# Two one-bank PSUM tiles for the products in place of the halves of one two-bank tile, and a new order of the first products

## The chip, the core and the metric

The kernel runs on one core of a Trainium2 chip. Its engines are TensorE (PE; its weight loads are shown apart as PEld), VectorE (DVE), ScalarE (ACT), GpSimd (POOL) and SyncE (SP, which here issues DMAs). The metric is the device time of one execution in microseconds (us). The measurement of this kernel repeats to about 0.2%.

## The reference

One call computes three things in fp32: attention in which a query sees only the keys of its hash bucket (2 batches, 8 heads, 768 positions, 64 wide), and two feed-forward blocks over 1536 tokens of width 512.

```
# attention: scores where the 6-bit buckets of q and k agree, else -1e9; softmax; times v
# first block (d_ff 1024)
a = x @ w1;  b = x @ w2
h = a * b @ w3
out_1 = h @ w_out
# second block (d_ff 1536)
g = x @ w_gate
silu = g * (1.0 / (1.0 + exp(-g)))
val = x @ w_val
out_2 = silu * val @ w_out
```

## The kernel before, in words

**Order of the work.** The kernel is written as small operations, each with candidate engines, an estimated cost, a priority and resources that it takes and gives back (slots of SBUF, PSUM tiles, temporaries). A planner (`Plan`) walks a model of time when the program is built, chooses an engine for each operation and fixes the order of each engine's queue. Semaphores are then put in by tile: an instruction that writes a tile waits for earlier readers of that tile and the like. Engines work their queues in order, so an instruction that waits holds back all behind it on its engine. TensorE's operations are chained in the order in which the code names them (`fill_op`), so the planner does not reorder products.

**Stages.** The attention fills the span to about 317 us, mixed with first pieces of the two blocks; until about 463 us the first third of the tokens goes through both blocks, and weights prepared there are kept in DRAM. Then `pair` handles the other two thirds together: `pair(1, ...)` the first block (about 463 to 598 us) and `pair(2, ...)` the second (598 to 797 us). The change works in these two calls.

**Exact products from fast ones.** An fp32 product is made of three fast matmuls on high and low parts (`split_mm`, L248 to L251). A *group* is such a triple: 128 weights columns, 512 columns moved. A low part is written by DVE or POOL at L262, a high part by ACT at L255.

**Sets.** In `pair` the tokens and weights are combined in the manner of Strassen: for each pair of column blocks `jp` and each `z` of 0 and 1 there is a *set* of seven products p1 to p7, of two groups each (q = 0 and 1), in place of eight. The first call has four `jp` (8 sets), the second six (12 sets). `wset` fetches two weight blocks (wA, wB) from DRAM and forms two sums of them (wP, wQ): two full adds (L1156), four quarter adds (L1167) on DVE or POOL, then high and low parts. `xset` does the like for the tokens (X1.., X2..; T1 to T4 are sums).

**Banks of the products.** Products accumulate in PSUM: p1 and p2 in tile `a`, p6 in `b` (one bank each, from two tiles tagged "one"). `cd` is one tile of 128x1024, two banks, one of three tagged "two"; p5 and p3 use its first half ("bank c"), p7 and p4 its second ("bank d"). After each product `after` has an eviction of 128x512 put out: ACT copies `a` to `u` (L1349); DVE adds `b` to `u`, then c to `u` gives `v` (p5), d to `v` gives part of G (p7), c to `u` (p3) and d to `u` (p4), all at L1321. Accumulation goes on: p3 adds to what p5 left in c, p4 to what p7 left in d, so p3 must wait for the eviction of p5, p4 for that of p7, and the next set's p5 and p7 for the evictions of p3 and p4. Products of G (L1334) and their splits (C) feed the second stage: *units* of one group on tiles `pacc`, of which `some` puts one behind p6, p2, p7 and p3 each, so that a regular set is p1 p6 unit p5 p2 unit p7 unit p3 unit p4, 54 matmuls. In the first set of a call there are no units yet, except that the first call begins with four units of the work before it (`lead`, tile `acc`; copies `ot` at L1083 take them out and a DMA stores each).

The order of the first two sets of a call is written out by hand in `pair`; before it is, as z then p: 01 11 02 12 05 07 06 16 03 04 15 17 13 14.

Of the kernel before, what the change touches and what calls it, by code (L numbers as in the profile page):

```python
# [28 lines left out]
NSLOT_MOE = 14  # L29
# [3 lines left out]
N_ST = 7  # L33
# [138 lines left out]
def moe_after_bucket_attention(ctx: ExitStack, tc: tile.TileContext, qk, vv, pp, cst, w12, w3t, w_out, wgv, wo2, out):  # L172
# [4 lines left out]
    psum = ctx.enter_context(tc.tile_pool(name="psum", bufs=1, space=bass.MemoryType.PSUM))  # L177
    ctx.enter_context(tc.manual_schedule())
    pools = {}
# [28 lines left out]
    env = {}  # L208
    uid = [0]

    def two(key):
        env[key] = psum.tile([128, 1024], F32, tag="two", name=key, bufs=3)
        return env[key]
# [225 lines left out]
    def head(hh):  # L439
# [74 lines left out]
        def bits():  # L514
            r = slice(QB0, KB0 + NM)
            DVE.tensor_scalar(  # L516
                out=q[r], in0=env.pop(f"proj{hh}")[r, 0:S], scalar1=thr[r], scalar2=val[r], op0=ALU.is_gt, op1=ALU.mult
            )
# [7 lines left out]
        def bits_k():  # L526
            r = slice(QB0, QB0 + NM)
            DVE.tensor_scalar(
                out=k[r], in0=env.pop("projk")[r, 0:S], scalar1=pr[r, 14:15], scalar2=pr[r, 15:16],
# [52 lines left out]
    def tile_ops(s):  # L582
# [11 lines left out]
        def clip():  # L594
            env[f"ms{s}"] = ap.tile([128, S], F32, tag="ms", name=f"ms{s}", bufs=N_MS)
            env[f"mx{s}"] = ap.tile([128, 2], F32, tag="mx", name=f"mx{s}", bufs=6)
            ps = env.pop(f"S{s}")
# [28 lines left out]
        def pe_second():  # L626
            v = env.pop(f"T{s}")[:, 0:S].rearrange("p (c q) -> p c q", c=6)
# [392 lines left out]
    def stage2(n, cdep):  # L1020
# [11 lines left out]
        for o_ in range(4):  # L1032

            def go(o_=o_):
                if first and at[o_][1] == 0:
                    two(ak + str(at[o_][0]))
# [25 lines left out]
            if kind == 1:  # L1062
# [13 lines left out]
            else:  # L1076

                def e1(eng, o_=o_):
                    def go():
# [155 lines left out]
    def pair(kind, nj, xdep, lead, gate, prio):  # L1235
# [8 lines left out]
        for jp in range(njp):  # L1244
            for z in range(2):
                w_of[jp, z] = wset(f"{kind}_{jp}_{z}", f"{kind}_{2 * jp}_{z}", f"{kind}_{2 * jp + 1}_{z}")
            if kind == 2:
                for j in (2 * jp, 2 * jp + 1):
                    wo_of[j] = fetch(f"wo2p_{j}", f"2_{j}_2", 1)
        if kind == 2:  # L1250
            for j in range(nj):
                wo_of[j, 2] = fetch(f"wo2q_{j}", f"2_{j}_2", 1)

        def prod(jp, z, p):
            key = f"{kind}_{jp}_{z}"
            wn, c0, xn = PROD[p]
            bank = {1: "a", 2: "a", 6: "b", 5: "c", 3: "c", 7: "d", 4: "d"}[p]
            begins = p in (1, 6, 5, 7)
            o = None
            for q in range(2):  # L1260

                def go(q=q):
                    if bank in "ab":
                        if begins and q == 0:
                            one(bank + key)
                        ps = env[bank + key]
# [14 lines left out]
                if begins and q == 0:  # L1281
                    if bank in "ab":
                        acq = [("F", 1)]
                    elif bank == "c":
                        deps.append(cd[0])
                        if cd[2] != kind:
# [19 lines left out]
        def after(jp, z, p, o):  # L1306
# [10 lines left out]
            def cdb(h):  # L1317
                return env["cd"][:, HALF[h]]
# [69 lines left out]
            elif p == 4:  # L1388
                rel = []
                if jp == njp - 1:  # L1390
                    rel = [("two", 1)]

                def go():
# [224 lines left out]
```

## Time and profile before

| | |
|---|---|
| median of 3 runs | 804.15 us (803.67 to 805.5) |
| profiled execution | 803.58 us, of which the span from first to last instruction is 801.8 us |
| mean granted TensorE clock | 0.997 |
| busy: PE, PEld, DVE, ACT, POOL | 761.0, 624.9, 539.3, 486.3, 332.9 us |
| matmul instructions | 3888 |

Read it as follows. Busy shares are means over stages of different limits; a busy TensorE counts overlapped durations, so the count of matmuls in a stretch tells more than the busy time. In the timeline a bracket behind a row gives the idle time before it on that engine and what ended it. Rows of 128x512 matmuls overlap: their starts stand closer together than they are long.

### The profile page before, as it was taken

The page shows a single profiled execution, that of the slowest core. Times are in us where ns is not written, and L with a number is a line of the kernel's source. Part 1 is how long each engine was busy: PE and PEld are TensorE (multiplying, and loading weights), DVE is VectorE, ACT ScalarE, POOL GpSimd, SP SyncE. Part 2 cuts the span into 40 slices and gives each one's busy share as a digit, 9 for nine tenths or more (in the row PEclk, how much of TensorE's full clock was granted, in tenths as well). Part 3 has the DMA queues.
Part 4 walks back from the last instruction along what each step waited for, and adds up shares of the span by engine and source line. Part 5 has one row for each costly group of instructions (what it writes and reads, how often), then busy time and mean ns, then how long its engine had stood idle before and what let it go on. Part 6 is the DMA issues. An engine that isn't in the chain of part 4 may idle for free.

```text
span 801.8 us, 11300 instructions
## 1 busy us (share of the span) xinstructions
PE 761.0 (95%) x3888; PEld 624.9 (78%) x3888; DVE 539.3 (67%) x929; ACT 486.3 (61%) x880; POOL 332.9 (42%) x321
## 2 busy tenths in 40 slices
PE   7998999999999899999999998999997899999997
PEld 5786888888888789787888875777785677777786
DVE  7888878878778987274378665566646675565450
ACT  7988989998789899698898832122332322322210
POOL 3676578575547553245421434232206123252000
PEclk9999999999999999999999999999999999999999
DMA  7794955774696862798888862212242333354211
GB/s 216 171 229 119 221 162 142 152 186 117 175 230 193 237 202 71 272 324 302 310 312 313 292 226 89 82 58 81 99 131 80 105 105 102 109 163 151 105 52 54
DMA packets 43329, 135.11 MB, mean 169 GB/s; under 512 B 7892, under 2 KB 10068, under 8 KB 43272
## 3 DMA queue, kind: packets, MB, share of 16 engines
q1 hardware_dynamic: 41032, 123.38, 48.3%
q0 software_dynamic: 2240, 11.01, 6.6%
q8 instruction: 31, 0.51, 0.3%
q14 instruction: 26, 0.21, 0.1%
HBM read 97.85 MB, written 30.46 MB: 160 GB/s over the span
## 4 chain that ended last, share of the span: by engine, by line
PE 67%; DVE 13%; ACT 8%; issue 5%; DMA 4%; POOL 2%; SPq 0%; POOLq 0%; ACTq 0%; DVEq 0%
PE cd L249 6%; PE T L620 5%; PE cd L251 4%; PE cd L250 4%; PE av L689 3%; PE av L690 3%; DVE sl_G L1321 3%; PE pacc_two L249 2%; PE pacc_two L251 2%; PE pacc_two L250 2%; PE S L591 2%; PE S L592 2%; PE a L249 2%; PE a L251 2%; PE a L250 2%
## 5 line engine op out<-in xcount | busy, mean ns | idle before, releaser
L598 DVE TENSOR_SCALAR_CACHE_REDUCE ms<-S 128x768 f32<-128x768 f32 x96 | 91.3, 951 | 20.5 <-PE S L592 13.8
L262 DVE TENSOR_TENSOR P<-T,P 128x768 fp32r<-128x768 f32 x96 | 91.0, 953 | 18.9 <-ACT P L624 18.1
L611 ACT ACTIVATE ms<-ms,mx 128x768 f32<-128x768 f32 x96 | 89.8, 936 | 6.2 <-DVE mx L605 5.7
L620 PE MATMUL T<-cs,ms 128*128 128x128 f32 x576 | 79.3, 274 | 3.3 <-ACT ms L611 1.0
L624 ACT CAST P<-T 128x768 fp32r<-128x768 f32 x96 | 76.1, 796 | 7.0 <-PE T L620 5.4
L689 PE MATMUL av<-P,VP 128*128 128x256 f32 x288 | 75.8, 297 | 0.6 <-ACT tt L700 0.3
L620 PEld LDWEIGHTS T<-cs,ms 128*128 128x128 f32 x576 | 65.3, 141 | 11.6 <-ACT ms L611 3.5
L690 PE MATMUL av<-P,VP 128*128 128x256 f32 x288 | 72.6, 286 | 0.8 <-DVE P L262 0.8
L591 PE MATMUL S<-KQ 128*128 128x512 f32 x192 | 67.8, 357 | 3.0 <-DVE ms L598 0.9
L592 PE MATMUL S<-KH,QL 128*128 128x512 f32 x192 | 60.5, 338 | 0.7 <-DVE QL L516 0.7
L689 PEld LDWEIGHTS av<-P,VP 128*128 128x128 f32 x288 | 55.4, 192 | 2.7 <-ACT tt L700 1.8
L690 PEld LDWEIGHTS av<-P,VP 128*128 128x128 f32 x288 | 55.6, 193 | 1.6 <-DVE P L262 1.2
L1349 ACT COPY u<-a 128x512 f32<-128x512 f32 x20 | 11.7, 586 | 72.0 <-PE a L251 71.9
L1167 POOL TENSOR_TENSOR sl_F<-sl_F 128x256 f32<-128x256 f32 x17 | 12.8, 756 | 84.8 <-DVE sl_F L1167 84.4
L262 POOL TENSOR_TENSOR sl_w2x<-sl_raww2x,sl_w2x 128x512 fp32r<-128x512 f32 x20 | 27.1, 1360 | 50.1 <-ACT sl_w2x L255 47.1
L255 ACT ACTIVATE dec_w2x<-sl_raww2x 128x512 f32<-128x512 f32 (+1 forms) x64 | 45.0, 728 | 3.9 <-DVE sl_raww2x L360 3.4
L591 PEld LDWEIGHTS S<-KQ 128*128 128x128 f32 x192 | 36.1, 188 | 12.1 <-DVE ms L598 3.2
L592 PEld LDWEIGHTS S<-KH,QL 128*128 128x128 f32 x192 | 36.2, 189 | 6.2 <-DVE QL L516 1.1
L360 DVE SCALAR_TENSOR_TENSOR sl_raww2x<-dec_w2x,dec_w2x 128x512 uint32<-128x512 uint32 x36 | 27.5, 764 | 16.9 <-ACT dec_w2x L255 16.2
L249 PE MATMUL m<-sl_X,sl_w2x 128*128 128x512 f32 x96 | 37.5, 390 | 1.4 <-ACT sa_m L902 1.4
L251 PE MATMUL m<-sl_X,sl_w2x 128*128 128x512 f32 x96 | 37.4, 389 | 0.0
L250 PE MATMUL m<-sl_X,sl_w2x 128*128 128x512 f32 x96 | 37.3, 389 | 0.0
(277 smaller groups left out, 2234.0 us busy)
## 6 DMA issues: line engine op xcount, KB each, us to landing
dram<-sl_w2x SPq DMA_DIRECT2D x36, 512.0 KB, 3.7
sl_raww2x<-in_wgv_dram SPq DMA_DIRECT2D x24, 512.0 KB, 6.2
KQ<-in_qk_dram POOLq DMA_DIRECT2D x28, 384.0 KB, 6.3
sl_wA<-dram SPq DMA_DIRECT2D x20, 512.0 KB, 4.2
sl_wB<-dram SPq DMA_DIRECT2D x20, 512.0 KB, 3.4
sl_raww<-in_w3t_dram SPq DMA_DIRECT2D x16, 512.0 KB, 4.8
sl_raww12f<-in_w_dram SPq DMA_DIRECT2D x16, 512.0 KB, 4.3
dram<-sl_w12f SPq DMA_DIRECT2D x16, 512.0 KB, 5.8
```

What stands on the lines that cost most here:

```text
L249: PE.matmul(ps, a_hi, b_hi, start=first, stop=False, skip_group_check=more)
L250: PE.matmul(ps, a_hi, b_lo, start=False, stop=False, skip_group_check=more)
L251: PE.matmul(ps, a_lo, b_hi, start=False, stop=last, skip_group_check=more)
L262: eng.tensor_tensor(out=out_, in0=a, in1=b, op=ALU.subtract)
L591: PE.matmul(ps[:, c0:c1], a[:, 0, qs], a[:, 1, c0:c1], start=True, stop=False)
L592: PE.matmul(ps[:, c0:c1], q[:, qs], k[:, c0:c1], start=False, stop=True)
L598: DVE.tensor_scalar(out=env[f"ms{s}"], in0=ps[:, 0:S], scalar1=-BIG, scalar2=None, op0=ALU.max, op1=ALU.max, accum_out=env[f"mx{s}"][:, 0:1],)
L611: ACT.activation(p, p, AF.Exp, bias=m[:, 1:2], scale=0.125, accum_out=env[f"sums{hh}"][:, qt : qt + 1])
L620: PE.transpose(ps[:, c * 128 : c * 128 + 128], p[:, c * 128 : c * 128 + 128], ident)
L624: ACT.copy(env[f"P{n}"][:, kk, 0:6], env[f"T{s}"][:, 0:S].rearrange("p (c q) -> p c q", c=6))
L689: PE.matmul(ps[:, 0:256], vab, p[:, :, c], start=c == 0, stop=False)
L690: PE.matmul(ps[:, 0:256], vab, p[:, :, 6 + c], start=False, stop=c == 5)
```

## The change

- `cd` is no longer one tile of two banks. The third of the "two" tiles lies in a pool of its own; when the first product on bank c comes, that pool is closed and a new one is opened in its place with two tiles of one bank, `c` and `d` (`bank_pair`, `bank`). They stay to the end of the second call.
- The "two" tiles are given out from an explicit list; accumulators that last never get the third.
- In the second call the units of the last pass use `c` and `d` in place of a "two" (`at1`).
- The products of the first two sets (first call) or the first four (second call, where two `jp` are interwoven) stand in a new order. The lead units of the first call follow the first product; before, they followed the third.
- Fetches of the second block's output weights are named behind the next `jp`'s weights; there are 15 slots for 14, and 5 temporaries for 7 (`N_ST`).

```diff
-NSLOT_MOE = 14
+NSLOT_MOE = 15
-N_ST = 7
+N_ST = 5
...
+    psum_c = tc.tile_pool(name="psum_c", bufs=1, space=bass.MemoryType.PSUM)
+    pools = {"two0": psum, "two1": psum, "two2": psum_c.__enter__()}
...
+    def bank_pair():
+        free_twos.remove("two2")
+        psum_c.__exit__(None, None, None)
+        pools["cd"] = ctx.enter_context(tc.tile_pool(name="psum_cd", bufs=1, space=bass.MemoryType.PSUM))
+
+    def bank(which, key):
+        env[key] = pools["cd"].tile([128, 512], F32, tag=which, name=key, bufs=1)
         return env[key]
...
-                        if "cd" not in env:
-                            two("cd")
-                        ps = env["cd"][:, HALF[bank == "d"]]
+                        if "cd" not in pools:
+                            bank_pair()
+                        if at not in env:
+                            bank(at, at)
+                        ps = env[at]
...
             def cdb(h):
-                return env["cd"][:, HALF[h]]
+                return env["cd"[h]]
...
-        at1 = [("one", 0, 0), ("one", 1, 0), ("two", 0, 0), ("two", 0, 1)]
+        at1 = [("one", 0, 0), ("one", 1, 0), *([("two", 0, 0), ("two", 0, 1)] if kind == 1 else [("c", 0, 0), ("d", 0, 0)])]
...
-                order = [(0, 1), (1, 1), (0, 2), (1, 2), (0, 5), (0, 7), (0, 6), (1, 6), (0, 3), (0, 4), (1, 5), (1, 7), (1, 3), (1, 4)]
+        if kind == 1:
+            seq = steps(0, "01 06 05 07 02 11 03 16 04 15 12 17 13 14 01' 06' 02' 05' 07' 03' 04' 11' 16' 15' 12' 17' 13' 14'")
+        else:
+            seq = steps(0, "01 11 02 12 01' 11' 02' 05 07 06 12' 16 03 04 15 17 06' 13 14 05' 07' 03' 04' 16' 15' 17' 13' 14'")
```

(A stroke marks the second `jp`.) What the change moves, in the order of three places; of each group only the first matmul stands, and "waits" names the engine whose semaphore is waited for.

TensorE in the first two sets of the first call, before: from the p3 of the first set on. `X1..` are parts of the tokens, `w..` of the weights.

```order
L249 MATMUL cd<-sl_X1B_166_4887,sl_wP_0_0_214_5412 128x512 [waits DVE_49]
...
L249 MATMUL cd<-sl_X1B_168_4897,sl_wP_0_0_214_5412 128x512 [waits DVE_49]
...
L249 MATMUL cd<-sl_X1T_197_5218,sl_wB_0_0_206_5324 128x512 [waits DMAHW7_49]
...
L249 MATMUL cd<-sl_X1T_198_5224,sl_wB_0_0_206_5324 128x512 [waits DVE_49]
...
L249 MATMUL cd<-sl_X1T_175_4985,sl_wQ_0_1_222_5494 128x512 [waits Activation_49]
...
L249 MATMUL cd<-sl_X1T_180_5032,sl_wQ_0_1_222_5494 128x512 [waits DVE_49]
...
L249 MATMUL cd<-sl_X1T_181_5034,sl_wQ_0_1_222_5494 128x512
...
L249 MATMUL cd<-sl_X1T_186_5097,sl_wQ_0_1_222_5494 128x512 [waits DVE_49]
```

Now, from the same p3 on:

```order
L268 MATMUL c<-sl_X1B_166_4890,sl_wP_0_0_215_5417 128x512 [waits DVE_49]
...
L268 MATMUL c<-sl_X1B_168_4900,sl_wP_0_0_215_5417 128x512
...
L268 MATMUL b_0_1_5519<-sl_X1T_190_5144,sl_wP_0_1_220_5491 128x512 [waits Activation_49]
...
L268 MATMUL b_0_1_5519<-sl_X1T_191_5154,sl_wP_0_1_220_5491 128x512
...
L268 MATMUL d<-sl_X1T_195_5191,sl_wB_0_0_206_5319 128x512 [waits DMAHW7_49]
...
L268 MATMUL d<-sl_X1T_199_5233,sl_wB_0_0_206_5319 128x512
...
L268 MATMUL c<-sl_X1T_175_4988,sl_wQ_0_1_223_5511 128x512 [waits DVE_49,Activation_49]
...
L268 MATMUL c<-sl_X1T_181_5037,sl_wQ_0_1_223_5511 128x512
...
L268 MATMUL a_0_1_5498<-sl_X1B_162_4844,sl_wA_0_1_209_5356 128x512 [waits Activation_49]
...
L268 MATMUL a_0_1_5498<-sl_X1B_163_4864,sl_wA_0_1_209_5356 128x512
...
L268 MATMUL d<-sl_X1T_182_5052,sl_wQ_0_1_223_5511 128x512 [waits DVE_49]
...
L268 MATMUL d<-sl_X1T_186_5102,sl_wQ_0_1_223_5511 128x512
```

The products of c and d stood next to each other, with a wait ahead of a second group, too (the sl_wP, wB and wQ rows with a wait in the middle of a product); now products on `a`, `b`, `c` and `d` take turns, and a wait stands only ahead of a product's first group.

VectorE in the same sets, before: from the low part of the first wP on.

```order
L262 TENSOR_TENSOR sl_wP_0_0_214_5412<-sl_F_0_0_209_5355,sl_wP_0_0_214_5412 128x512 [waits Activation_49]
L262 TENSOR_TENSOR sl_wQ_0_0_216_5434<-sl_F_0_0_209_5355,sl_wQ_0_0_216_5434 128x512 [waits Activation_49]
L1167 TENSOR_TENSOR sl_F_0_1_215_5414<-sl_F_0_1_215_5414 128x256 [waits DMAHW4_49,Pool_49]
L1167 TENSOR_TENSOR sl_F_0_1_215_5414<-sl_F_0_1_215_5414 128x256 [waits DVE_49] x3
L1321 TENSOR_TENSOR sl_G_1_0_217_5440<-a_0_1_5416,sl_G_1_0_217_5440 128x512 [waits PE_49,Activation_49]
L262 TENSOR_TENSOR sl_wP_0_1_220_5477<-sl_F_0_1_215_5414,sl_wP_0_1_220_5477 128x512 [waits DMAHW0_49,Activation_49]
L262 TENSOR_TENSOR sl_C1p_0_221_5488<-sl_G_1_0_217_5440,sl_C1p_0_221_5488 128x512 [waits Activation_49]
L262 TENSOR_TENSOR sl_wQ_0_1_222_5494<-sl_F_0_1_215_5414,sl_wQ_0_1_222_5494 128x512 [waits Activation_49]
```

Now, from the same low part on:

```order
L281 TENSOR_TENSOR sl_wP_0_0_215_5417<-sl_F_0_0_210_5363,sl_wP_0_0_215_5417 128x512 [waits Activation_49]
L1106 COPY ot_1_5434<-acc_0_0_4581 128x512 [waits Activation_49]
L281 TENSOR_TENSOR sl_wQ_0_0_216_5436<-sl_F_0_0_210_5363,sl_wQ_0_0_216_5436 128x512 [waits DMAHW4_49,DMAHW0_49,Activation_49]
L1190 TENSOR_TENSOR sl_F_0_1_214_5411<-sl_F_0_1_214_5411 128x256 [waits Pool_49]
L1190 TENSOR_TENSOR sl_F_0_1_214_5411<-sl_F_0_1_214_5411 128x256 [waits DVE_49]
L1348 TENSOR_TENSOR u_0_0_5422<-b_0_0_5443,u_0_0_5422 128x512 [waits PE_49]
L1106 COPY ot_3_5475<-acc_0_1_4594 128x512 [waits DMAHW6_49,Activation_49]
L1348 TENSOR_TENSOR v_0_0_5477<-c,u_0_0_5422 128x512 [waits DVE_49,PE_49]
L1348 TENSOR_TENSOR sl_G_1_0_219_5489<-d,v_0_0_5477 128x512 [waits DMAHW0_49,DVE_49,PE_49]
```

Two of the four copies `ot` of the lead units, which ACT made before, stand on VectorE now, the second with a wait for a DMA; behind it stand the evictions of p5 (`v`) and p7. The eviction of p6 (`u`) has moved up ahead of the next set's splits.

TensorE at the head of the second call, before (of each product the first matmul):

```order
L249 MATMUL a_0_0_6315<-sl_X2B_288_6214,sl_wA_0_0_258_5944 128x512 [waits DMAHW5_49,Activation_49]
...
L249 MATMUL a_0_1_6327<-sl_X2B_288_6214,sl_wA_0_1_267_6035 128x512 [waits DMAHW7_49,Activation_49]
...
L249 MATMUL a_0_0_6315<-sl_X2B_291_6231,sl_wA_0_0_258_5944 128x512 [waits Activation_49]
...
L249 MATMUL a_0_1_6327<-sl_X2B_291_6231,sl_wA_0_1_267_6035 128x512 [waits Activation_49]
...
L249 MATMUL cd<-sl_X2T_293_6270,sl_wQ_0_0_275_6104 128x512 [waits DVE_49]
...
L249 MATMUL cd<-sl_X2T_298_6339,sl_wQ_0_0_275_6104 128x512 [waits DVE_49]
...
L249 MATMUL b_0_0_6388<-sl_X2T_302_6371,sl_wP_0_0_272_6082 128x512 [waits Activation_49]
...
L249 MATMUL b_0_1_6404<-sl_X2T_302_6371,sl_wP_0_1_281_6181 128x512
...
L249 MATMUL cd<-sl_X2B_296_6324,sl_wP_0_0_272_6082 128x512 [waits DVE_49]
...
L249 MATMUL cd<-sl_X2T_306_6395,sl_wB_0_0_264_6006 128x512 [waits DMAHW6_49,Activation_49]
```

Now:

```order
L268 MATMUL a_0_0_6336<-sl_X2B_288_6222,sl_wA_0_0_258_5938 128x512 [waits DMAHW5_49,Activation_49,Pool_49]
...
L268 MATMUL a_0_1_6351<-sl_X2B_288_6222,sl_wA_0_1_267_6032 128x512 [waits DMAHW7_49,Activation_49]
...
L268 MATMUL a_0_0_6336<-sl_X2B_292_6238,sl_wA_0_0_258_5938 128x512 [waits Activation_49]
...
L268 MATMUL a_0_1_6351<-sl_X2B_292_6238,sl_wA_0_1_267_6032 128x512 [waits Activation_49]
...
L268 MATMUL a_1_0_6389<-sl_X2B_288_6222,sl_wA_1_0_276_6126 128x512 [waits DMAHW1_49,Activation_49]
...
L268 MATMUL a_1_1_6403<-sl_X2B_288_6222,sl_wA_1_1_298_6321 128x512 [waits DMAHW3_49,DVE_49]
...
L268 MATMUL a_1_0_6389<-sl_X2B_292_6238,sl_wA_1_0_276_6126 128x512 [waits Activation_49]
...
L268 MATMUL c<-sl_X2T_294_6284,sl_wQ_0_0_274_6099 128x512
...
L268 MATMUL d<-sl_X2T_303_6366,sl_wQ_0_0_274_6099 128x512
...
L268 MATMUL b_0_0_6451<-sl_X2T_308_6396,sl_wP_0_0_271_6073 128x512 [waits Activation_49]
...
L268 MATMUL a_1_1_6403<-sl_X2B_292_6238,sl_wA_1_1_298_6321 128x512
...
L268 MATMUL b_0_1_6473<-sl_X2T_308_6396,sl_wP_0_1_280_6177 128x512 [waits DVE_49]
```

The first products of the second `jp` (a_1_0, a_1_1) have come in between; the products on `c` and `d` start later, and `b`, which needs the token sums T2, later still.

## Rows read from the trace of the kernel before

**Rows 1.** The page: TensorE busy in 40 slices, and the clock granted to it
```profile
PE   7998999999999899999999998999997899999997
...
PEclk9999999999999999999999999999999999999999
```

**Rows 2.** Busy time by stretch: start:end, length, five engines (count), PEclk, DMA, GB/s
```profile
480.00:500.00 20.00, 16.09 (x66) 11.63 (x65) 11.09 (x16) 3.89 (x7) 8.10 (x8) 1.00 0.26 91
500.00:520.00 20.00, 19.64 (x82) 14.87 (x81) 12.07 (x20) 2.85 (x6) 5.57 (x5) 1.00 0.31 100
580.00:600.00 20.00, 20.00 (x90) 16.49 (x89) 8.73 (x13) 7.64 (x15) 1.87 (x2) 1.00 0.44 144
600.00:620.00 20.00, 15.21 (x61) 10.71 (x60) 14.03 (x20) 6.98 (x13) 13.24 (x12) 1.00 0.25 82
```

**Rows 3.** Waits from 464 us on: waiter, waited for, total us, times, longest
```profile
PEld cd L249 <- DVE sl_G L1321: 14.4, 21, 1.2
...
PEld cd L249 <- DVE v L1321: 11.3, 14, 1.4
```

**Rows 4.** Timeline, first set of the first pair: start, duration, engine, instruction [idle <-releaser]
```profile
477.80 0.39 PE L251 MATMUL cd<-sl_X1B,sl_wP 128*128 128x512 f32 x1
478.22 0.69 DVE L1321 TENSOR_TENSOR sl_G<-cd,v 128x512 f32<-128x512 f32 x1 [0.42 <-PE cd L251]
...
478.97 0.50 PE L249 MATMUL cd<-sl_X1B,sl_wP 128*128 128x512 f32 x1 [0.78 <-DVE sl_G L1321]
```

**Rows 5.** Timeline, a later set, and the same matmul one set on
```profile
500.42 0.69 DVE L1321 TENSOR_TENSOR sl_G<-cd,v 128x512 f32<-128x512 f32 x1 [1.42 <-PE cd L251]
...
500.68 0.40 PE L251 MATMUL pacc_two<-sl_C1p,sl_WP 128*128 128x512 f32 x1
...
501.16 0.51 PE L249 MATMUL cd<-sl_X1B,sl_wP 128*128 128x512 f32 x1
...
514.23 0.50 PE L249 MATMUL cd<-sl_X1B,sl_wP 128*128 128x512 f32 x1
```

**Rows 6.** Timeline, TensorE in the second pair's first two sets
```profile
608.12 0.50 PE L250 MATMUL b<-sl_X2T,sl_wP 128*128 128x512 f32 x1 [1.15 <-DVE sl_X2T L262]
...
610.65 0.50 PE L249 MATMUL cd<-sl_X2B,sl_wP 128*128 128x512 f32 x1 [0.42 <-DVE v L1321]
...
627.15 0.50 PE L249 MATMUL b<-sl_X2T,sl_wP 128*128 128x512 f32 x1 [1.20 <-ACT sl_wP L255]
...
628.43 0.50 PE L251 MATMUL b<-sl_X2T,sl_wP 128*128 128x512 f32 x1 [0.55 <-DVE sl_wP L262]
...
649.77 0.50 PE L249 MATMUL cd<-sl_X2B,sl_wP 128*128 128x512 f32 x1 [0.93 <-DVE v L1321]
```

**Rows 7.** Timeline: splits and evictions beside GpSimd, and copies that wait for a DMA
```profile
465.11 1.28 POOL L1156 TENSOR_TENSOR sl_F<-sl_wB 128x512 f32<-128x512 f32 x1 [1.80 <-DMA sl_wB<-dram]
...
465.41 1.52 DVE L262 TENSOR_TENSOR sl_wP<-sl_F,sl_wP 128x512 fp32r<-128x512 f32 x1 [0.76 <-ACT sl_wP L255]
...
466.99 0.69 DVE L262 TENSOR_TENSOR sl_wQ<-sl_F,sl_wQ 128x512 fp32r<-128x512 f32 x1
...
471.86 0.59 ACT L1083 COPY ot<-acc 128x512 f32<-128x512 f32 x1 [1.31 <-DMA out_dram<-ot]
...
476.09 1.28 POOL L1156 TENSOR_TENSOR sl_F<-sl_wB 128x512 f32<-128x512 f32 x1 [9.71 <-DMA sl_wB<-dram]
476.48 0.69 DVE L1321 TENSOR_TENSOR v<-cd,u 128x512 f32<-128x512 f32 x1
...
605.65 1.81 DVE L262 TENSOR_TENSOR sl_XF<-sl_XF 128x512 f32<-128x512 f32 x1
```

**Rows 8.** Timeline, the end
```profile
796.94 0.39 PE L251 MATMUL pacc_two<-sl_wo2q,sl_C2p 128*128 128x512 f32 x1
797.37 0.58 ACT L1495 COPY sl_otp<-pacc_two 128x512 f32<-128x512 f32 x1 [1.45 <-PE pacc_two L251]
797.98 0.69 DVE L1495 COPY sl_otp<-pacc_two 128x512 f32<-128x512 f32 x1 [1.28 <-ACT sl_otp L1495]
```

More of the change, by code (lines that the diff above doesn't have):

```diff
@@ L209, in moe_after_bucket_attention, with two, end_two @@
     uid = [0]
-    def two(key):
-        env[key] = psum.tile([128, 1024], F32, tag="two", name=key, bufs=3)
+    free_twos, two_of = deque(["two0", "two1", "two2"]), {}
+    def two(key, lasting=False):
+        tag = two_of[key] = next(x for x in free_twos if not lasting or x != "two2")
+        free_twos.remove(tag)
+        env[key] = pools[tag].tile([128, 1024], F32, tag=tag, name=key, bufs=1)
+        return env[key]
+    def end_two(key):
+        free_twos.append(two_of.pop(key))
+        return env.pop(key)
+    def bank_pair():
[4 more added lines that the diff above has]
+        env[key] = pools["cd"].tile([128, 512], F32, tag=which, name=key, bufs=1)
         return env[key]
@@ L1437, in acc, with open_acc @@
                 return env[ak + what + str(z)][:, HALF[hf]]
+            def open_acc(o_):
+                what, z, hf = at[o_]
+                if hf == 0 and what in "cd":
+                    bank(what, ak + what + str(z))
+                elif hf == 0:
+                    (two if what == "two" else one)(ak + what + str(z))
             def unit(o_):
@@ L1442, in go @@
                 def go():
-                    if first and hf == 0:
-                        (two if what == "two" else one)(ak + what + str(z))
+                    if first:
+                        open_acc(o_)
                     ps, c, w = acc(o_), env[k], env[wname]
@@ L1454, in go @@
                             drop(wname)
-                acq = [("two" if what == "two" else "F", 1)] if first and hf == 0 else []
+                acq = [("two" if what == "two" else "F", 1)] if first and hf == 0 and what not in "cd" else []
+                deps = [cdep, wdep, sw]
+                if first and what in "cd":
+                    deps.append(cd["cd".index(what)])
                 rel = [(c_res(j, h), 1)] if o_ == 3 else []
@@ L1471, in out_block, with end_acc @@
             what, z, hf = at[o_]
-            rel = [("F", 1)] if what == "one" else ([("two", 1)] if o_ == 3 or at[o_ + 1][:2] != (what, z) else [])
+            ends = what == "two" and (o_ == 3 or at[o_ + 1][:2] != (what, z))
+            rel = [("F", 1)] if what == "one" else [("two", 1)] if ends else []
+            def end_acc():
+                if ends:
+                    end_two(f"pacc{kind}_{h}_{what}{z}")
             prev = out_prev.get((h, what, z))
@@ L1514, in pair, with steps @@
         at0 = [("two", 0, 0), ("two", 0, 1), ("two", 1, 0), ("two", 1, 1)]
[L1515 to L1528 removed]
+        at1 = [("one", 0, 0), ("one", 1, 0), *([("two", 0, 0), ("two", 0, 1)] if kind == 1 else [("c", 0, 0), ("d", 0, 0)])]
+        def steps(jp, text):
+            return [(jp + (x[2:] == "'"), int(x[0]), int(x[1])) for x in text.split()]
+        if kind == 1:
+            seq = steps(0, "01 06 05 07 02 11 03 16 04 15 12 17 13 14 01' 06' 02' 05' 07' 03' 04' 11' 16' 15' 12' 17' 13' 14'")
+        else:
+            seq = steps(0, "01 11 02 12 01' 11' 02' 05 07 06 12' 16 03 04 15 17 06' 13 14 05' 07' 03' 04' 16' 15' 17' 13' 14'")
+        done = 2
+        seq += [(jp, z, p) for jp in range(done, njp) for z in range(2) for p in (1, 6, 5, 2, 7, 3, 4)]
+        for n, (jp, z, p) in enumerate(seq):
+            prod(jp, z, p)
+            if n == 0 and kind == 1:
+                some(len(units))
+            if p in (6, 2, 7, 3):
+                some()
+            if (z, p) == (1, 4):
+                some(len(units))
+                if jp < njp - 1:
+                    for j in (2 * jp, 2 * jp + 1):
+                        units.extend(s2_units(j, 0, at0))
         passes = ((0, 1), (2, 3)) if kind == 1 else ((0, 1, 2, 3),)
```

66 lines of the change are left out of this document (27 added, 39 removed).

## The prediction

> **What bounds the kernel now.** First I read the slices of the page [rows 1]: TensorE is at nine tenths or more nearly everywhere, at full granted clock, with dips at both ends and at three places behind 480 us. So I asked for stretches and counted matmuls [rows 2]. At 580 to 600 us, where only second-stage units run, 90 matmuls start in 20 us: one per 0.222 us; on the starts of undisturbed neighbours it is 0.227, and I use that as the full rate. The pair stages miss it: 66 at 480 to 500 us, 82 at 500 to 520, 61 at 600 to 620 (some records can be missing, so the counts are a guide and the sum below goes by gaps). No other engine is full there (DVE 11 to 14 of 20 us). What TensorE waits for, the list of waits tells [rows 3]: its weight loads onto `cd`, for DVE evictions, never for longer than 1.4 us.
>
> One such wait is to be seen in [rows 4]. The matmul at 477.80 ends the first group of p3 on the first half of `cd`. DVE then makes part of G from `cd` and `v`: the eviction of p7, which reads the other half. It begins only 0.42 us after that matmul's start, though p7 was done long before, and the second group of p3 begins at 478.97, 1.17 us after the last matmul instead of 0.23. Both instructions use one tile in two banks and neither needs what the other touches. So the halves are made to take turns because they are one tile. The bare cycle is then 0.42 + 0.69 + 0.06 = 1.17 us for an eviction to come between two groups.
>
> **The change part by part.** The sum is made in the frame of the profiled execution, 803.58 us (span 801.8 and 1.78 around it); the median shown, 804.15, lies 0.57 above.
>
> *Two tiles for one.* (a) Where no unit stands between, a false turn costs 1.17 - 0.23 = 0.94 us, and 0.11 more because the matmul after a stop starts 0.34 later and not 0.23: 1.05 us [rows 4]. I count 13 such gaps in the timeline: six from 478.97 to 491.18 (the first call's first two sets), five from 612.41 to 622.23 (the second call's), and 649.77 and 653.59 (the first of those two in [rows 6]). 13 x 1.06 = 13.8 us. (b) In regular sets a unit of three matmuls lies between and covers part: 500.68 to 501.16 is 0.48 instead of 0.23, with the slow restart 0.36 us [rows 5]. Two in a set, 12 in the first call and 18 in the second: 30 x 0.36 = 10.8 us. As a check, the same matmul stands 13.07 us later one set on (514.23 - 501.16), and 54 matmuls at 0.227 are 12.25; two gaps explain 0.72 of the 0.82 between. The 0.1 left I keep in the time. (c) What takes their place: p3 now waits for the eviction of p5 only, p4 for that of p7, and the next set's p5 and p7 for those of p3 and p4. In the regular order 12 matmuls or more (2.7 us) lie between a product and the one that needs its eviction, against 1.17. That is cover, unless DVE is busy with something else just then; it works 11 to 14 of 20 us [rows 2], in pieces mostly of 0.4 to 0.7. For 20 sets I put 0.5 us, between 0 and 2. Sum of this part: -13.8 - 10.8 + 0.5 = -24.1.
>
> *The new order of the first sets.* In the old order TensorE also met true waits: 608.12 for the split of the token sum T2 (1.15 idle, with restart and the part that the load shows 1.42), 610.65 for `v` (0.69), 627.15 and 628.43 for wP of the second `jp` (1.48 and 0.82) [rows 6], and 477.22 and 465.90 (0.41 and 0.36), 5.2 us together. In the new order `b` of the second call, which needs T2, stands 54 matmuls behind the head and not 36, that is 4 us later, and in the built order VectorE, and no longer GpSimd, forms the late set's sums and their low parts ahead of the token splits, some 4 us of work in a stretch where it is busy 8.7 of 20 [rows 2]; I take all 5.2 as gone. What the order adds has to be bounded at two places. First call: its `b` is needed about 467.0 instead of 474.2 (6 products' matmuls and 12 lead matmuls behind 462.92), and the low part of wP it needs ended at 466.93 before, having taken 1.52 [rows 7]: 0 to 0.7 us late. On VectorE the second copy `ot` now waits for the output DMA of the first; on ScalarE this wait ended at 471.86 [rows 7]. Behind it in DVE's queue stand `v` and p7's eviction, for which p3 waits at about 473.8. If the copy starts at 471 there is a microsecond to spare, if at 473 the loss is 2. Also, the sums of the second weights set hang on a POOL add that waited 9.71 us for a load [rows 7], and DVE's last quarter add for them now stands ahead of p7's eviction for p4. Together 0 to 3, and I take 0.7, since the copy's row lies in time. Second call: from `b` on, products that depend on one another over a bank have only one product of six matmuls (1.36 us) between them, against 1.17 for the eviction: 0.2 of slack, some ten times. DVE has there besides the token splits, mostly 0.69 but once 1.81 [rows 7]; one that is slow costs about a microsecond when it stands in front of an eviction. 0 to 4 us, taken 1.5: two such slips. Sum of this part: -5.2 + 0.7 + 1.5 = -3.0.
>
> One rule bears on that size. The row at 465.41 is a split of two SBUF tiles beside a POOL add, 1.52 instead of 0.69; the row at 476.48 is an eviction (one PSUM input and one SBUF input) beside a POOL add, and takes 0.69 all the same [rows 7]. The Trainium skill says the same in "SBUF — State Buffer", section "Who interferes with whom": a DVE instruction with at most one SBUF input does not contend with GpSimd, one with two does against a GpSimd instruction that reads SBUF. By that rule and by the row evictions are not stretched, and my 1.5 stands; if they were stretched as splits are, 0.83 each, ten of them would make it 8.
>
> *The end.* The last copy on DVE (797.98) waits for ACT's copy of the other half of the same tile (797.37), and the output DMA waits for it [rows 8]. With `c` and `d` apart both start behind their own last matmul: -0.6 us, between 0 and -0.7.
>
> *What I cost at nothing.* Two "two" tiles suffice in the pair stages, since only two accumulators last; closing the pool waits for the readers of its last tile, long done at the first product on `c`. One slot more and two temporaries fewer: the temporaries that turn round are given back by the same evictions that now come sooner. The output-weight fetches, behind the next set's weights on SP's queue, are first needed some 130 matmuls (30 us) after the call's head; DMA is busy 0.25 to 0.44 [rows 2]. If they came late, units of the second stage would wait, at a microsecond or two each time.
>
> Sum: -24.1 - 3.0 - 0.6 = -27.7 us; 803.58 - 27.7 = 775.9, and 776.4 in the frame of the median.
>
> **The rivals.**
> 1. *VectorE takes the place of the false waits at the heads.* For it: the new order makes a chain of evictions with 0.2 us of slack, and more adds and splits compete. Against: DVE is idle 6 to 9 of 20 us there, and the queue orders put evictions mostly in front. Price: if each of the ten chained products of the second call loses 1.05 as before, and the first call's copy and add cost their 3: 13.5 instead of 2.2, so 776.4 + 11.3 = 787.7; half of it gives 782.
> 2. *The halves still take turns* (the change doesn't do what it says). Then the 10.8 of regular sets remains, and of the 13.8 the part that the alternating order doesn't hide, perhaps half: 776.4 + 10.8 + 6.9 = 794. Against: in the built order the second groups have no wait any more, and the tiles are separate.
> 3. *Slower: the weights come late.* The quarter adds, high and low parts for wP are made set by set by POOL, DVE and ACT, and TensorE takes sets 0.85 us sooner each; POOL makes 28 quarter adds for 17 now. A late wP cost 2.3 us at 627.15 and 628.43 [rows 6]. Once in each of 18 sets would be 41 us, so 776.4 + 41 = 817; it decides from 12 sets on (12 x 2.3 = 27.7). Against: it happened once in 20 sets, and POOL is busy 4 to 13 of 20 us. A faster TensorE can't outrun it by much, since a set still takes 12.3 us.
>
> **How the numbers follow.** Forecast, 0.80: 776, with its own range from 772 (no new waits, and the 0.1 of each set gone too: 776.4 - 2.7 - 2) to 783 (all bounds at their far ends: 9 us for 2.7). Rival 1, 0.13: 782 to 788. Rival 2, 0.03: 794. Rival 3, 0.03: 817. Something not seen, 0.01. The range is 772 to 785: it leaves out the upper part of rival 1 and the others, and no more. Faster by over 0.2% (1.6 us, about what a measurement of this kernel can tell from no change): forecast, rival 1 and rival 2, 0.96. Within it 0.01, slower 0.03.
>
> **What would show it.** Right: no wait of TensorE for an eviction in regular sets, the same matmul 12.3 us on and not 13.07; 86 to 90 matmuls in the stretches from 500 us on; the first call's first unit of the second `jp` about 6 us earlier against its head; DVE's last copy no longer behind ACT's. Wrong: new idle rows of TensorE on `c`, `d`, `b` in the second call's first four sets behind DVE splits or sums (rival 1); rows of TensorE on `b` that wait for wP in many sets (rival 3); waits of 0.36 in regular sets as now (rival 2). A granted clock below that of [rows 2] in these stretches would overturn the sum, too.

## The result and the profile after

The changed kernel takes 771.87 us (median of 4, 771.44 to 772.38) against 804.83 us of the kernel before on the same chip (median of 4): a ratio of 0.9589, 95% interval 0.9568 to 0.9610. The forecast was 776 with a range of 772 to 785: the direction and the mechanism held, but the gain of 33 us was larger than the 27.7 of the sum, and the time lies 0.13 us under the range. That distance is less than the runs differ among themselves (one of the four took 772.38), and the 0.2% that I had named for the repeats is too small: in the measurements of the experiments below, the kernel before took from 799.79 to 808.0 us. The profiled execution took 771.44 us, its span is 769.4.

The page of the changed kernel, the span, TensorE's 40 slices and its granted clock, as in [rows 1]:

```profile
span 769.4 us, 11284 instructions
...
PE   7988999999999899999999999999999999999997
...
PEclk9999999999999999999999999999999999999999
```

The dips behind 480 us are gone; what is left stands in the stages ahead of the change and at the very end. The stretches that answer to [rows 2] (length, then busy time and count of PE, PEld, DVE, ACT, POOL, then granted clock, DMA share, GB/s):

```profile
480.00:500.00 20.00, 20.00 (x89) 16.46 (x89) 15.48 (x23) 6.41 (x11) 11.42 (x11) 1.00 0.29 96
500.00:520.00 20.00, 20.00 (x90) 16.57 (x89) 14.42 (x23) 3.59 (x7) 4.52 (x5) 1.00 0.27 89
580.00:600.00 20.00, 20.00 (x89) 16.54 (x89) 13.26 (x19) 9.10 (x17) 4.93 (x4) 1.00 0.50 165
600.00:620.00 20.00, 19.67 (x87) 15.81 (x87) 16.60 (x25) 7.23 (x12) 13.16 (x13) 1.00 0.40 132
```

The stretches are the same by the clock, so they hold partly different work. TensorE is full in three of four and starts 89, 90, 89 and 87 matmuls where it started 66, 82, 90 and 61. In the first, second and fourth, DVE has gone from 11 to 14 us busy in 20 to between 14 and 16.6: it makes the same evictions in less time. The list of waits from 462 us on now holds for TensorE only these rows, where [rows 3] had 14.4 and 11.3 us:

```profile
PEld d L268 <- DVE u L1348: 0.7, 1, 0.7
PE d L268 <- DVE u L1348: 0.3, 1, 0.3
PEld d L268 <- DVE sl_G L1348: 0.2, 1, 0.2
```

In a regular set the eviction of p7 (504.68, from `d`) now runs while TensorE goes from the unit into p3 on `c` without a stop, and the same matmul stands 12.24 us on (517.34 - 505.10), not 13.07 as in [rows 5]; 54 matmuls at 0.227 are 12.25. The first unit of the second `jp` starts 24.49 us after the first product (486.64) where it took 31.80 before (494.72), so 7.3 us earlier, and I had said about 6. Timeline of the changed kernel:

```profile
504.68 0.68 DVE L1348 TENSOR_TENSOR v<-d,v 128x512 f32<-128x512 f32 x1
504.87 0.39 PE L270 MATMUL pacc_two<-sl_C1p,sl_WP 128*128 128x512 f32 x1
505.10 0.39 PE L268 MATMUL c<-sl_X1B,sl_wP 128*128 128x512 f32 x1
...
517.34 0.39 PE L268 MATMUL c<-sl_X1B,sl_wP 128*128 128x512 f32 x1
```

Where did the 32.14 us between the two profiled executions go? The first product of the first call and the last matmul bound the stage that the change works in. Before, it began here, and ended with the 796.94 row of [rows 8]:

```profile
462.92 0.39 PE L249 MATMUL a<-sl_X1B,sl_wA 128*128 128x512 f32 x1
```

After:

```profile
462.15 0.39 PE L268 MATMUL a<-sl_X1B,sl_wA 128*128 128x512 f32 x1
...
765.10 0.39 PE L270 MATMUL pacc_d<-sl_wo2q,sl_C2p 128*128 128x512 f32 x1
```

That is 334.02 us before and 302.95 after: -31.07 for the same 1332 matmuls, which at 0.227 take 302.1. From the last matmul to the span's end (769.37 to the hundredth) 4.86 became 4.27 (-0.59), the start of the stage, behind code that the change hardly touches, came 0.77 earlier, and the time around the span is 2.07 and not 1.78 (+0.29).

The one stop left, of 0.72 us from start to start, is this one, at the place that rival 1 named:

```profile
610.12 1.28 POOL L281 TENSOR_TENSOR sl_wP<-sl_F,sl_wP 128x512 fp32r<-128x512 f32 x1
...
610.33 1.63 DVE L1361 TENSOR_TENSOR sl_G<-sl_G,t 128x512 f32<-128x512 f32 x1
...
610.53 0.39 PE L270 MATMUL d<-sl_X2T,sl_wB 128*128 128x512 f32 x1
...
611.88 0.68 DVE L1348 TENSOR_TENSOR u<-d,u 128x512 f32<-128x512 f32 x1
611.89 0.39 PE L270 MATMUL c<-sl_X2T,sl_wQ 128*128 128x512 f32 x1
...
612.61 0.50 PE L268 MATMUL d<-sl_X2T,sl_wQ 128*128 128x512 f32 x1 [0.33 <-DVE u L1348]
```

The first matmul of a product on `d` waits at 612.61 for the eviction that began at 611.88. That eviction stood in DVE's queue behind a multiplication of two SBUF tiles, which lasted 1.63 us beside a GpSimd instruction (610.12 to 611.40) in place of 0.69. TensorE stood still because the multiplication was ahead, as the run with that multiplication made later shows (below).

### The profile page after: what moved, and what is told of

It is laid out like the page before. It is cut to its first block, busy times and chain, and to the rows that moved or that the text cites. A ratio compares the mean times of both kernels' runs of the same rounds, so it can differ in the third digit from the quotient of the medians.

```text
span 769.4 us, 11284 instructions
## 1 busy us (share of the span) xinstructions
PE 746.2 (97%) x3888; PEld 627.8 (82%) x3888; DVE 544.5 (71%) x927; ACT 484.6 (63%) x878; POOL 338.0 (44%) x325
## 4 chain that ended last, share of the span: by engine, by line
PE 75%; ACT 9%; DVE 6%; DMA 3%; POOL 3%; issue 3%; SPq 1%; ACTq 0%; POOLq 0%; DVEq 0%
PE T L639 5%; PE pacc_two L268 3%; PE pacc_two L269 3%; PE pacc_two L270 3%; PE av L708 3%; PE av L709 3%; PE m L268 3%; PE m L270 3%; PE m L269 3%; PE a L268 2%; PE a L270 2%; PE a L269 2%; PE d L268 2%; PE c L270 2%; PE c L268 2%
## 5 line engine op out<-in xcount | busy, mean ns | idle before, releaser
L708 PE MATMUL av<-P,VP 128*128 128x256 f32 x288 | 74.7, 293 | 0.8 <-ACT P L643 0.4
L709 PE MATMUL av<-P,VP 128*128 128x256 f32 x288 | 71.5, 283 | 0.8 <-DVE P L281 0.8
L708 PEld LDWEIGHTS av<-P,VP 128*128 128x128 f32 x288 | 54.6, 190 | 2.9 <-ACT tt L719 1.8
L709 PEld LDWEIGHTS av<-P,VP 128*128 128x128 f32 x288 | 54.8, 190 | 1.6 <-DVE P L281 1.2
L281 POOL TENSOR_TENSOR sl_w2x<-sl_raww2x,sl_w2x 128x512 fp32r<-128x512 f32 x22 | 29.7, 1353 | 58.3 <-ACT sl_w2x L274 58.3
L1190 POOL TENSOR_TENSOR sl_F<-sl_F 128x256 f32<-128x256 f32 x28 | 23.7, 845 | 62.2 <-DVE sl_F L1190 60.3
```

What stands on the lines that cost most here:

```text
L281: eng.tensor_tensor(out=out_, in0=a, in1=b, op=ALU.subtract)
L708: PE.matmul(ps[:, 0:256], vab, p[:, :, c], start=c == 0, stop=False)
L709: PE.matmul(ps[:, 0:256], vab, p[:, :, 6 + c], start=False, stop=c == 5)
```

## The experiments

The stage from the first product to the last matmul (its first and last rows in the timeline, as above) is the yardstick: it repeats, while the time ahead of it doesn't. "Start" is when the stage began. The medians come from several chips; beside the experiments the kernel before had medians of 802.79 us, 804.03 and, in one run, 801.32, and the ratios given are to the one on the same chip.

| kernel | start, us | stage, us | median, us |
|---|---|---|---|
| before; once more | 462.92; 463.95 | 334.02; 334.18 | 804.83 |
| after; once more | 462.15; 460.82 | 302.95; 302.98 | 771.87 |
| split alone (old orders) | 459.60 | 308.44 | 777.05 |
| new orders alone (joint tile) | 461.71 | 328.74 | 798.53 |
| old order in the second call | 461.28 | 305.80 | 774.04 |
| old order in the first call | 464.68 | 305.74 | 774.76 |
| lead units after the third product | 466.28 | 305.67 | 778.09 |
| old sizes | 465.76 | 302.77 | 771.21 |
| multiplication later | 459.44 | 302.18 | 770.54 |
| 60 evictions twice | 463.43 | 306.51 | 775.49 |
| 60 evictions three times | 464.68 | 327.80 | 798.66 (one run) |

**The split alone.** The changed kernel with the old orders:

```diff
-            seq = steps(0, "01 06 05 07 02 11 03 16 04 15 12 17 13 14 01' 06' 02' 05' 07' 03' 04' 11' 16' 15' 12' 17' 13' 14'")
+            seq = steps(0, "01 11 02 12 05 07 06 16 03 04 15 17 13 14 01' 06' 05' 02' 07' 03' 04' 11' 16' 15' 12' 17' 13' 14'")
...
-            if n == 0 and kind == 1:
+            if n == 2 and kind == 1:
                 some(len(units))
```

(the same line for the second call.)

> The changed kernel with the old order of the first two sets in both calls and the lead units after the third product; the split into c and d, the sizes and the order of the fetches are kept. Theory (the separate tiles do it): the false turns stay away, only the true waits of the old order come back (608.12, 610.65, 627.15 and 628.43, 477.22 of the kernel before, 4.8 us, between 2 and 7): 774 to 779 us, and no wait of TensorE in regular sets. Rival (the new order does it, by putting products on other banks between): the heads' 13.8 us come back as well, 788 to 792.

Measured: 777.05 us, ratio 0.9662 (0.9620 to 0.9705); stage 308.44. The theory holds: regular sets show no stop, and the heads (the first sets of each call) show true waits, as these on TensorE at the second call's head (for a token sum, and for `v`, as in [rows 6]):

```profile
594.30 0.50 PE L269 MATMUL b<-sl_X2T,sl_wP 128*128 128x512 f32 x1 [0.72 <-DVE sl_X2T L281]
...
595.51 0.50 PE L269 MATMUL b<-sl_X2T,sl_wP 128*128 128x512 f32 x1 [0.24 <-DVE sl_X2T L281]
...
599.13 0.50 PE L268 MATMUL c<-sl_X2B,sl_wP 128*128 128x512 f32 x1 [1.51 <-DVE v L1348]
```

The split by itself brings 334.02 - 308.44 = 25.58 us.

**The new orders alone.** `c` and `d` are halves of one tile again:

```diff
 def bank_pair():
...
+    env["both"] = pools["cd"].tile([128, 1024], F32, tag="both", name="both", bufs=1)
...
-        env[key] = pools["cd"].tile([128, 512], F32, tag=which, name=key, bufs=1)
+        env[key] = env["both"][:, HALF[which == "d"]]
```

> The changed kernel with c and d as the two halves of one tile of two banks again, in the pool of the new tiles; order, sizes and the last pass on c and d are kept. Theory (separate tiles): 0.36 us comes back twice in each regular set (30 times, 10.8 us), the last copy waits for the other half again (0.6), and the alternating heads lose something between 1 and 5: 783 to 789 us. Rival (the new order does it): 772 to 776, with waits in regular sets only where DVE is late.

Measured: 798.53 us, ratio 0.9939 (0.9913 to 0.9966); stage 328.74. The false turns are back, in regular sets as in [rows 5] (timeline, the tile is named `both`; DVE's eviction of p7, the end of the unit, the next product):

```profile
497.06 0.69 DVE L1349 TENSOR_TENSOR sl_G<-both,v 128x512 f32<-128x512 f32 x1 [1.06 <-PE both L271]
...
497.33 0.39 PE L271 MATMUL pacc_two<-sl_C1p,sl_WP 128*128 128x512 f32 x1
...
497.81 0.50 PE L269 MATMUL both<-sl_X1B,sl_wP 128*128 128x512 f32 x1
```

and in the list of waits, which is close to that of [rows 3]:

```profile
PEld both L269 <- DVE v L1349: 12.9, 14, 2.0
PEld both L269 <- DVE sl_G L1349: 11.9, 19, 1.2
...
PEld both L269 <- DVE t L1349: 5.4, 9, 1.2
```

The theory's 783 to 789 us and the rival's 772 to 776 were both too low. I had reckoned 1 to 5 us for the heads, since products on `a` and `b` stand between there. But many products on `c` and `d` still follow each other directly, and the two halves then take turns: eleven stops of 1.17 us or more stand in the heads, where the kernel before had 13 false turns. The new orders by themselves bring 5.28 us, about the 5.2 of true waits, and hide next to nothing of the false ones. 25.58 + 5.28 = 30.86 is nearly the 31.07 of both: the two parts of the change add up, and the first is five sixths of it. Both runs also keep the rest of the change (the sizes, the later fetches, the last pass on `c` and `d`), which so counts twice in 30.86; with parts that simply add, that rest comes to -0.21 us (30.86 - 31.07), next to nothing.

**The old order in one call at a time.**

> The changed kernel with the old order of products in the first sets of the second call only. Theory (separate tiles): the two true waits for T2 and v come back (1.4 and 0.7 us) and perhaps that for wP (2.3, if the planner makes it late again): 773.5 to 776.5 us. Rival (the new order does it): also the five false turns of 1.06 there and the two at 649.77 and 653.59: 781 to 784.

> The changed kernel with the old order of products and the old place of the lead units in the first call only. Theory (the split does most, the orders remove true waits): from the first product to the last matmul 302.95 us become 304.5 to 306.5, since the true waits of the old order there (for the copy u, and for v twice; 2.1 us in the run with both old orders, and slow restarts) come back: 773 to 776 us. Rival (the new order hides false turns): 308 or more, 778 or more.

Measured: second call's old order 774.04 us, ratio 0.9633 (0.9594 to 0.9671), stage 305.80, 2.85 more than the changed kernel; its stops are the three of the run with the split alone. First call's old order 774.76 us, ratio 0.9626 (0.9577 to 0.9675), stage 305.74, 2.79 more. The two add up to 5.64, and both old orders together cost 5.49. Both totals are as the theory has it. The single waits are not: in the second call's old order the wait for `v` took 1.51 us idle where it had taken 0.42 before, and that for wP, which the theory had left open, did not come.

**The place of the lead units.**

```diff
-            if n == 0 and kind == 1:
+            if n == 2 and kind == 1:
                 some(len(units))
```

> The changed kernel with the lead units after the third product again, as before. Theory (the copies ot on DVE have 1 us to spare in the changed kernel): b is asked for earlier than wP is ready or the copies reach v, so the stretch from first product to last matmul grows by 0 to 2 us. Rival (the place of the lead units decides the first call's head): 3 us or more.

Measured: 778.09 us, ratio 0.9662 (0.9611 to 0.9713); stage 305.67, 2.72 more, nearer to the rival than to the theory. The timeline shows why (DVE makes the low part of wP, TensorE waits with `b` for its high and its low part):

```profile
469.03 1.61 DVE L281 TENSOR_TENSOR sl_wP<-sl_F,sl_wP 128x512 fp32r<-128x512 f32 x1 [0.76 <-ACT sl_wP L274]
469.05 0.50 PE L268 MATMUL b<-sl_X1T,sl_wP 128*128 128x512 f32 x1 [1.25 <-ACT sl_wP L274]
...
470.69 0.50 PE L270 MATMUL b<-sl_X1T,sl_wP 128*128 128x512 f32 x1 [0.91 <-DVE sl_wP L281]
```

Here `b` follows the first product directly. It is due 1.4 us after the stage's start, begins at 2.8 and stops once more, 2.5 us late in all. In the changed kernel the 12 lead matmuls stand in between and cover it. It was the weights that needed the cover, not the copies `ot`.

**The sizes** (14 slots and 7 temporaries as before).

> The changed kernel with 14 slots and 7 temporaries as before, in place of 15 and 5. The prediction costed these at nothing. Theory: first product to last matmul 302.95 within 1 us. Rival (a load or a weight comes late without the slot): 2 us or more, with waits on b for wP or on a and d for loads.

Measured: 771.21 us, ratio 0.9590 (0.9540 to 0.9640); stage 302.77, 0.18 less. They cost nothing in either direction, as put.

**How much DVE can take.** The evictions of p5 and p3, and of p7 and p4 where z is 0, are made twice or three times; they write the same result again, so what is computed stays.

```diff
+            def tt2(out_, a, b, alu):
+                tt(out_, a, b, alu)
+                tt(out_, a, b, alu)
...
-                ready[jp, z, 3] = st_ops[jp, z, "v"] = evict(5, lambda: tt(st(vn), cdb(0), env[u], ALU.add), [o, st_ops[jp, z, "U"]], acq=[("st", 1)])
+                ready[jp, z, 3] = st_ops[jp, z, "v"] = evict(5, lambda: tt2(st(vn), cdb(0), env[u], ALU.add), [o, st_ops[jp, z, "U"]], acq=[("st", 1)])
...
```

> The changed kernel with 60 of the 80 DVE evictions of c and d made twice, one straight behind the other (those of p5 and p3, and of p7 and p4 where z is 0: they do not overwrite what they read), so that a bank is held 0.6 us longer and DVE works some 37 us more. It measures the slack that the prediction took as small. Theory (much slack): 12 matmuls (2.72 us) still cover 0.42 + 1.30 in regular sets, only the heads with one product between lose, 0.4 us some ten times: 772 to 777. Rival (DVE was close to being the bound, which is what the prediction priced at 2.7 us): 785 or more, with waits in regular sets too.

> As the run with evictions twice, but three times in a row: a bank is held 1.2 us longer and DVE works some 73 us more in 20 sets. For one bank 12 matmuls (2.72 us) still cover 0.42 + 0.69 + 1.22 + 0.06 = 2.39; but DVE, 17 to 18 of 20 us busy with evictions twice in the first call's regular sets, would need some 20 to 21. Theory (the bound in regular sets is DVE's whole work, not the single eviction): now stops in regular sets of the first call, few in those of the second, and the stretch from first product to last matmul goes from 306.5 to between 312 and 325 us. Rival (cover per bank decides): regular sets stay at full rate, 308 to 311.

Measured: twice 775.49 us, ratio 0.9653 (0.9607 to 0.9699), stage 306.51, 3.56 more. Stretches of that run:

```profile
500.00:520.00 20.00, 20.00 (x90) 16.55 (x89) 16.95 (x26) 4.66 (x8) 6.35 (x6) 1.00 0.30 102
600.00:620.00 20.00, 18.48 (x78) 13.84 (x77) 19.11 (x29) 5.01 (x9) 12.16 (x12) 1.00 0.29 101
```

In the regular sets TensorE stays at 90 matmuls with DVE at 16.95 of 20 us; the loss lies in the second call's head, in five stops from 604.05 to 628.29 (78 matmuls at 600 to 620 us). Three times: 798.66 us in one run, stage 327.80:

```profile
500.00:520.00 20.00, 19.78 (x85) 15.91 (x86) 19.04 (x33) 4.45 (x8) 6.58 (x7) 1.00 0.16 53
540.00:560.00 20.00, 17.73 (x72) 14.12 (x71) 19.52 (x28) 3.95 (x8) 7.95 (x7) 0.91 0.15 53
555.00:560.00 5.00, 4.70 (x14) 3.71 (x15) 4.83 (x9) 0.06 (x1) 1.77 (x2) 0.66 0.01 2
```

With DVE at 19 and more of 20 us in most stretches the regular sets stop as well, though the larger part of the stops still stands in the heads. So what rival 1 describes does happen once DVE has enough work: 3.56 us of it with 37 us of work more than the change leaves, and its price of 5.6 to 11.3 us (782 to 788 against 776.4) is reached somewhere between 37 and 73. The signs of the theory for the second run came (four stops in regular sets of the first call, two in those of the second). That DVE's whole work sets the bound there, and not the single late eviction, is argued and not shown: at 560 to 580 us DVE is busy for 19.00 us and TensorE still starts 89 matmuls. The stage came out 2.8 us over the range given, for the reason in the last section.

**The last stop.** One multiplication behind p4's eviction:

```diff
             elif p == 3:
...
-                st_ops[jp, 3, "m"] = times(3, t, o, [("st", 1)])
+                if kind == 1 or jp:
+                    st_ops[jp, 3, "m"] = times(3, t, o, [("st", 1)])
...
             elif p == 4:
...
+                if kind == 2 and jp == 0:
+                    st_ops[jp, 3, "m"] = times(3, t, o, [("st", 1)])
                 st_ops[jp, 4, "m"] = times(4, u, o, [("st", 1)])
```

> The changed kernel with one multiplication of the second call's first set (G times t) made behind the eviction of p4 and not ahead of it. In the changed kernel TensorE has one stop, 0.72 us at 612.61, for an eviction of d that stands in DVE's queue behind this multiplication of two SBUF tiles, which took 1.63 us beside a GpSimd instruction in place of 0.69. Theory: that stop goes and nothing else moves, 302.95 becomes 302.4; it is the price of rival 1 where it occurs. Rival (DVE is full there): the stop stands at another place with the same length. The time is within 0.3% of the changed kernel either way.

Measured: 770.54 us, ratio 0.9603 (0.9542 to 0.9663); stage 302.18. The stop is gone; the eviction (608.25) starts 0.42 us after the last matmul's start, and `d` goes on at full rate:

```profile
607.83 0.39 PE L270 MATMUL d<-sl_X2T,sl_wB 128*128 128x512 f32 x1
608.25 0.69 DVE L1348 TENSOR_TENSOR u<-d,u 128x512 f32<-128x512 f32 x1 [0.67 <-PE d L270]
...
608.86 1.05 DVE L1361 TENSOR_TENSOR sl_G<-sl_G,t 128x512 f32<-128x512 f32 x1
...
609.41 0.39 PE L268 MATMUL d<-sl_X2T,sl_wQ 128*128 128x512 f32 x1
```

The stage is 0.77 us shorter and stands at the full rate of 302.1. In the whole time, which scatters more, that is no measurable gain over the changed kernel.

**The repeats.**

> The changed kernel once more, unchanged. In the runs so far the first product of the first call began between 459.4 and 466.3 us after code that is the same in all of them. If that scatter belongs to the executions, the stretch from first product to last matmul repeats within 0.5 us of 302.95, wherever it begins.

> The kernel before once more, unchanged: the stretch from first product to last matmul repeats within 0.5 us of 334.02, wherever it begins.

Measured: 302.98 and 334.18 us for the stage, within 0.2 of the first profiles. The start of the stage went from 459.44 to 466.28 us over all runs of the table, though the code ahead of it is the same or nearly so. So the stage is sure to tenths of a microsecond, and the scatter of the whole time comes from ahead of it. Part of that is TensorE's clock: the run that began the stage first (459.44) shows a mean granted clock of 1.000 for its span, one that began it at 464.68 shows 0.993. But starts of 459.60 and 466.28 go with 0.997 and 0.996, so the clock is not all of it, and the rest is open.

## Why the prediction was right, and where not

The mechanism was right. Two terms of the sum were mis-sized, and both made the forecast too long: the new waits (2.7 us put in, 0.6 measured) and the rest of 0.1 us per set that was left in the time (1.5 of it went).

- **That the halves took turns because they were one tile: right.** Split alone 25.58 us, joint tile 25.79 back (328.74 - 302.95). The sum had 24.1 for it, after 0.5 of new waits.
- **The true waits at the heads, 5.2 us, all gone: right**, since none of them is left in the changed kernel. 5.28 by the new orders alone and 5.49 on top of the split agree with the 5.2, but that is partly luck: with the old orders and separate tiles the two waits for wP (2.3 us) did not come back, while those for `v` and `u` were longer (`v` 1.51 us idle and not 0.42).
- **The end, -0.6: right**, -0.59; with the joint tile the last matmul stands 4.88 us ahead of the end again. ACT's copy and DVE's now follow their own last matmul. Ahead of them in this timeline stands the last matmul, behind it DVE's copy, 0.42 after its start:

```profile
764.84 0.59 ACT L1530 COPY sl_otp<-pacc_c 128x512 f32<-128x512 f32 x1 [0.78 <-PE pacc_c L270]
...
765.10 0.39 PE L270 MATMUL pacc_d<-sl_wo2q,sl_C2p 128*128 128x512 f32 x1
765.52 0.69 DVE L1530 COPY sl_otp<-pacc_d 128x512 f32<-128x512 f32 x1 [0.67 <-PE pacc_d L270]
```

- **The new waits, 2.7 us: the first step that failed by size.** They came to 0.6, one stop. For the first call's head I had 0.7: it cost nothing. The copy `ot` came at 470.57, near the 471 that I had reckoned, and p3 at 473.03 found `v` ready; the low part of wP took 0.69 and not the 1.52 of [rows 7]:

```profile
464.90 0.69 DVE L281 TENSOR_TENSOR sl_wP<-sl_F,sl_wP 128x512 fp32r<-128x512 f32 x1 [0.76 <-ACT sl_wP L274]
...
470.57 0.69 DVE L1106 COPY ot<-acc 128x512 f32<-128x512 f32 x1 [2.03 <-ACT ot L1104]
471.18 0.68 DVE L1348 TENSOR_TENSOR v<-c,u 128x512 f32<-128x512 f32 x1
...
473.03 0.39 PE L268 MATMUL c<-sl_X1B,sl_wP 128*128 128x512 f32 x1
```

For the second call's head I had 1.5, two slips; there was one, of 0.6. For regular sets 0.5; there was none. The run with evictions twice shows how much room there was: regular sets and the first call's head took 0.6 us more on each bank without a stop, and only the second call's chained head had little.
- **The rest of 0.1 us per set, kept in the time: wrong, the second step that failed.** It went with the stops: the same matmul is now 12.24 us on. Neighbours without a stop between (starts 0.20 to 0.26 us apart) stand 0.2271 apart on average in the changed kernel and stood 0.2283 before, 1.5 us over 1233 of them. Nearly all of it lies just behind the stops: of these neighbours before, the 338 among the first ten behind a stop average 0.2314, the other 895 average 0.2271. So beside the wait and the one slow restart a stop costs another 0.03 us in the matmuls that follow; why they stand further apart is open. With a 0.5 us difference in the sizes of the stops (30.3 us measured before, 29.8 in the sum) that makes 1.9 us. The check that left 0.1 unexplained was the hint: what a stop costs is better taken from the period (0.82 a set) than from the two gaps alone (0.72).
- **The part ahead of the change** came 0.77 us earlier in this profile. It wasn't in the sum, and by the table it scatters by 7 us between executions. So 2.1 + 1.9 + 0.8 less 0.3 around the span make the 4.5 us between the sum (775.9) and the profiled time. The range had no room for this scatter at its low end, which was the bare sum without new waits (771.7, rounded up).
- **Rival 1** occurred once, in the form named. The rule of the Trainium skill that was weighed there ("SBUF — State Buffer", section "Who interferes with whom") agrees with the rows of the one stop: the multiplication of two SBUF tiles started at 610.33, while GpSimd held until 611.40, and ended at 611.96, 0.56 us behind; all 110 evictions with one SBUF input kept their 0.68 to 0.69. **Rival 2** would have come to 798.5 instead of the 794 I gave: the heads keep nearly all their turns. **Rival 3** did not occur: no row of waits on `b` for wP is left in the changed kernel. But the run with the lead units third shows its price, 2.5 us once, close to the 2.3 taken from [rows 6].

## What to carry to other kernels

Where a scheduler puts in semaphores by tile, two banks that are filled and emptied independently should be two tiles: here products on one half waited 43 times for the eviction of the other, 1.05 us where nothing stood between and 0.36 with one group between, and splitting the tile took this away without a change of order. The engine named as releaser in such a row need not be slow; ask first whether the two instructions touch the same data at all. When a stop recurs in a loop, take its cost from the period of the loop, and give the range of a forecast the scatter of the parts that the change does not touch.

## What the runs showed of the hardware that I had not expected

With evictions three times, TensorE lost more than the waits, and the granted clock tells how. Timeline of TensorE around the longest stop, in which it stood still for 2.27 us:

```profile
552.63 0.39 PE L270 MATMUL pacc_two<-sl_C1p,sl_WP 128*128 128x512 f32 x1
...
555.30 0.50 PE L268 MATMUL d<-sl_X1T,sl_wB 128*128 128x512 f32 x1 [2.27 <-DVE sl_G L1348]
...
557.03 0.63 PE L270 MATMUL d<-sl_X1T,sl_wB 128*128 128x512 f32 x1
557.45 0.63 PE L268 MATMUL a<-sl_X1B,sl_wA 128*128 128x512 f32 x1
...
559.74 0.39 PE L268 MATMUL b<-sl_X1T,sl_wP 128*128 128x512 f32 x1
```

From 556.17 on matmuls start 0.43 us apart and not 0.23, until 559.16: the stretch 555 to 560 us above has a granted clock of 0.66, which mixes the two levels of 2.4 and 1.2 GHz. The same followed the stops of 1.79 us at 479.70 and of 1.93 us at 630.46, but not that of 1.78 at 690.06, nor any of the stops of up to 1.2 us before the change, where the clock stood at 1.00 in the stretches with the most stops [rows 2]. So each of these three stops cost about 1.6 us more than itself, 4.8 us in all, and without that the stage would lie within the range given for it. "TensorE: Matmul & The Clock Gate" of the Trainium skill (section "A second HAM failure mode: psum-queue depth-cycling") names frequent idle moments between groups of matmuls as a cause of such throttling, in a bf16 kernel. In this case the 49 short stops of the kernel before show none. What decides which stop is followed by the lower level no run here shows.
